# Reordering the first four attention steps of a fused dilated attention and gated unit kernel

## The chip, the cores and the metric

The kernel runs on one core of one Trainium2 chip. The metric is the device time of one execution in microseconds (us); of several runs of one kernel the median is given.

## The reference

The inputs q, k and v have 8 batches, 8 heads, 576 positions and 64 elements a head, in float32. Heads 0 to 3 attend to the last 32 positions; heads 4 to 7 attend to every fourth of the last 128. The heads' outputs are laid side by side and go through a gated unit with a causal convolution of 5 taps.

```python
scores = scale * q @ k^T                       # per batch and head, 576 x 576
mask_plain = (rel >= 0) & (rel < 32)           # heads 0-3
mask_dil = (rel >= 0) & (rel < 128) & (rel % 4 == 0)   # heads 4-7
attn = softmax(where(mask, scores, -1e9))
x = concat_heads(attn @ v)                     # 8 x 576 x 512
gate = sigmoid(causal_depthwise_conv(x, conv_w))       # 5 taps, per channel
out = (gate * (x @ w_val)) @ w_out             # 8 x 576 x 512
```

## The kernel before, in words

The work is cut into 32 steps, i = 0 to 31. A step is a pair of heads of one batch; four steps make a batch, and its channels 128c to 128c+127 (c = i % 4) are the pair's output. Two pairs form a group g: even groups hold heads 0 to 3 (plain), odd groups heads 4 to 7 (dilated). pair_info gives batch, c, kind, group and the place a of the pair in its group. The order of instructions on every engine is the order in which the program issues them; no scheduler changes it, and the queues are first in, first out.

Loads go through SP's queue in the order of issue (load_main for the first 512 positions of k or q, load_rest for the other 64, load_v for v). Groups 0 and 1 are loaded ahead of the loop, half of group 0's q by ACT's queue; groups 2 and 3 by pairs in steps 0 to 3, group 4 in step 3, and each later group two or so steps apart, three groups ahead. The pool of k_nat, q_nat and qk_rest has four buffers of each name. conv_w (conv_nat, 10 KB) is loaded by GpSimd's queue, as are w_val (step 1) and w_out (step 3), which are cast on the way.

Plain k and q are first cast to bf16 and reordered (cast, L171): group 0's first pair by VectorE (k) and ScalarE (q), its second pair by ScalarE inside step 0, and later groups by GpSimd, where these casts stand in one queue with the casts of v for dilated steps (prep_v, L183: vA and vB). In particular the casts of group 4's k are issued in step 4 and prep_v(6) in step 5.

trans_main (L321) transposes k or q of one or both pairs of a group on TensorE into a PSUM bank of the pool ps_one (four banks), and ScalarE copies the result out (for q of group 0: VectorE). trans_rest (L362) does so for the last 64 positions, with VectorE's copies. next_pair(i) (L579) does both for the pair of step i+1. From step 7 on, the transposes are made a whole group ahead.

A step runs scores (L390: for each half hf 6 matmuls into ps_sc, of which there are two, then an exp on ScalarE), apply_mask (L417: VectorE multiplies the exponentials by the mask), attn_v (L425: 6 matmuls of each half; both halves write into the ps_sc of half 1), and normalize (L446: reciprocal and product on VectorE). scores(i+1, 1) needs the ps_sc that normalize(i) reads. In the step after, after_x (L588) transposes the result (trans_x, VectorE copies it to xT) and appends two convolutions of the chunk to a list; pop_conv (L569) issues the first of that list when it is due. The convolution (L490) is a sum of matmuls with diagonal weights conv_diag[c], made by make_conv_diag(c) (L308) on VectorE from ident and conv_w_sb; setup_conv_w (L298) gets conv_w_sb by four small transposes on TensorE. run_val, val (L519) and out_tile (L535) are the products with w_val and w_out; they begin with steps 4 and 6. warm(n) (L573) issues n matmuls on constant data whose result is not used; they stand at the start and in steps 0 to 3.

make_mask_d builds the mask of dilated steps on GpSimd at the start, finish_mask_d ends it on VectorE in step 0. EARLY is 7, NCH is 4.

The softmax here doesn't subtract the row's maximum and nothing guards it: scores larger than these inputs give would overflow.

## Time and profile before

| what | value |
| --- | --- |
| median of 6 runs | 185.12 us (182.31 to 186.0) |
| the profiled execution | 182.72 us |
| its span in the profile | 181.0 us |
| PE (matmul) busy | 164.4 us, 91% |
| VectorE (DVE) busy | 119.0 us, 66% |
| ScalarE (ACT) busy | 120.4 us, 67% |
| GpSimd (POOL) busy | 42.0 us, 23% |
| moved by DMA | 42.28 MB, 234 GB/s over the span |
| start of scores(i, 0), i = 0 to 6 | 8.95, 13.34, 18.21, 22.98, 27.58, 32.32, 36.96 us |

All times in the profile are counted from the start of the span. PEld is TensorE's loading of weights. L508 is line 508 of the kernel. "SPq" and "ACTq" are the instructions with which SP and ACT issue DMAs; "out<-in" names the tile that is written and those that are read. A line of a timeline has start, duration, engine, line, operation, tiles, shape and count; the bracket at its end gives the idle time of the engine before it and what ended it. A slice is a fortieth of the span, here 4.525 us, and a digit the busy share in tenths.

### The profile page before, as it was taken

What the parts mean: (1) busy time and instruction counts of PE and PEld (TensorE: products, weight loads), DVE (VectorE), ACT (ScalarE), POOL (GpSimd) and SP (SyncE); (2) the same over time, 40 slices, a digit from 0 to 9 for tenths busy, and PEclk for the clock granted to TensorE, in tenths of its full rate; (3) what the DMA queues carried; (4) which work ended last, traced back from release to release, by engine and by line L of the source; (5) the groups of instructions that cost most, each with busy time, mean ns of one, the idle gap of its engine ahead of it and who ended that gap; (6) DMA issues with size and microseconds to landing.
All of it is one profiled execution on the core that took longest, in us unless ns stands there. A gap on an engine that the chain in (4) does not pass through costs nothing.

```text
span 181.0 us, 5175 instructions
## 1 busy us (share of the span) xinstructions
PE 164.4 (91%) x2029; PEld 119.7 (66%) x2057; DVE 119.0 (66%) x283; ACT 120.4 (67%) x217; POOL 42.0 (23%) x88
## 2 busy tenths in 40 slices
PE   5786777879999999999999999999999999999990
PEld 1445555657777777777777776777777777776650
DVE  3587466775677767577877776677877766774430
ACT  3266666658777777877877777777777778653341
POOL 6706420054054005300350054003600500000000
PEclk9999999999999999999999999999999999999999
DMA  5999999999999999999999999999997213112345
GB/s 151 259 277 307 217 251 302 304 268 283 329 268 229 295 327 267 211 314 325 279 246 286 332 277 216 319 316 287 217 296 258 71 58 116 62 58 63 116 126 163
DMA packets 62632, 42.28 MB, mean 234 GB/s; under 512 B 31371, under 2 KB 57995, under 8 KB 62608
## 3 DMA queue, kind: packets, MB, share of 16 engines
q1 hardware_dynamic: 60976, 40.57, 84.0%
q0 software_dynamic: 1088, 1.06, 3.6%
q8 instruction: 16, 0.26, 0.6%
q10 hardware_dynamic: 544, 0.33, 0.6%
q14 instruction: 8, 0.07, 0.1%
HBM read 33.56 MB, written 9.44 MB: 238 GB/s over the span
## 4 chain that ended last, share of the span: by engine, by line
PE 74%; SPq 11%; DMA 9%; issue 1%; POOL 1%; ACT 0%; DVE 0%; POOLq 0%; ACTq 0%
PE ps_bank L508 19%; PE ps_bank L538 17%; PE ps_bank L523 16%; SPq L115 7%; PE ps_bank L332 6%; PE ps_sc L441 6%; PE ps_sc L411 5%; DMA qk_rest<-in_k_dram 4%; DMA k_nat<-in_k_dram 3%; DMA q_nat<-in_q_dram 3%; PE ps_bank L469 2%; PE ps_bank L482 2%; SPq L148 1%; PE ps_bank L476 1%; PE ps_bank L367 1%
## 5 line engine op out<-in xcount | busy, mean ns | idle before, releaser
L508 PE MATMUL ps_bank<-xT,conv_diag 128*128 128x288 bf16 (+1 forms) x384 | 50.1, 266 | 2.0 <-DVE xT L484 2.0
L414 ACT ACTIVATE et<-ps_sc 128x576 bf16<-128x576 f32 x64 | 38.7, 648 | 6.7 <-PE ps_sc L411 4.2
L523 PE MATMUL ps_bank<-xT,w_val_b 128*128 128x288 bf16 x256 | 41.8, 286 | 0.4 <-DVE xT L484 0.4
L543 ACT ACTIVATE osb<-ps_bank 128x512 f32<-128x512 f32 x36 | 21.5, 597 | 25.1 <-PE ps_bank L538 21.8
L516 ACT ACTIVATE gate<-ps_bank 128x288 bf16<-128x288 f32 x64 | 26.7, 418 | 16.5 <-PE ps_bank L508 15.8
L508 PEld LDWEIGHTS <-conv_diag 128*128 128x128 bf16 x384 | 32.0, 97 | 8.4 <-issue 1.4
L529 DVE SCALAR_TENSOR_TENSOR y_all<-gate,ps_bank 128x288 bf16<-128x288 bf16 x64 | 28.9, 452 | 11.0 <-PE ps_bank L523 6.7
L538 PE MATMUL ps_bank<-w_out_b,y_all 128*128 128x512 bf16 x117 | 34.2, 379 | 1.4
L457 DVE TENSOR_TENSOR xn<-ps_sc,rec 96x768 bf16<-96x768 f32 (+1 forms) x32 | 30.6, 955 | 1.1
L523 PEld LDWEIGHTS <-w_val_b 128*128 128x128 bf16 x256 | 23.6, 98 | 10.1
L181 POOL CAST k_b<-k_nat 128x512 bf16<-128x512 f32 x14 | 8.9, 660 | 79.9 <-DMA k_nat<-in_k_dram 41.9
L441 PEld LDWEIGHTS <-et 128*128 128x128 bf16 x384 | 20.2, 98 | 5.2 <-DVE et L423 1.9
L452 DVE RECIPROCAL rec<-ps_sc 96x12 f32<-96x12 f32 (+1 forms) x32 | 7.4, 231 | 24.7 <-PE ps_sc L441 24.7
L484 DVE COPY xT<-ps_bank 128x576 bf16<-128x576 bf16 x32 | 14.6, 458 | 11.7 <-PE ps_bank L482 7.0
L538 PEld LDWEIGHTS <-y_all 128*128 128x128 bf16 x144 | 12.5, 97 | 10.9 <-DVE y_all L529 0.9
L423 DVE TENSOR_TENSOR et<-et,mask_p 128x576 bf16<-128x576 bf16 x32 | 15.9, 499 | 0.2 <-ACT et L414 0.2
L188 POOL CAST vA<-v_st 128x512 bf16<-128x512 f32 x16 | 10.9, 684 | 17.5 <-PE ps_sc L411 10.7
L423 DVE TENSOR_TENSOR et<-et,mask_d 128x576 bf16<-128x576 bf16 x32 | 15.0, 473 | 0.0
L441 PE MATMUL ps_sc<-vP,et 128*128 128x65 bf16 x192 | 11.4, 195 | 0.1
L347 ACT COPY kT<-ps_bank 128x1024 bf16<-128x1024 bf16 (+1 forms) x10 | 8.5, 848 | 4.2 <-PE ps_bank L332 4.2
L441 PE MATMUL ps_sc<-vA,et 128*128 128x65 bf16 x128 | 9.3, 194 | 0.4 <-POOL vA L188 0.4
L411 PE MATMUL ps_sc<-qT,kT 64*128 64x96 bf16 x192 | 7.5, 209 | 2.4 <-DVE qT L342 1.1
(82 smaller groups left out, 187.2 us busy)
## 6 DMA issues: line engine op xcount, KB each, us to landing
k_nat<-in_k_dram SPq DMA_DIRECT2D x12, 512.0 KB, 5.5
q_nat<-in_q_dram SPq DMA_DIRECT2D x12, 512.0 KB, 6.6
vP<-in_v_dram SPq DMA_DIRECT2D x6, 768.0 KB, 7.9
v_st<-in_v_dram SPq DMA_DIRECT2D x6, 512.0 KB, 6.5
k_nat<-in_k_dram SPq DMA_DIRECT2D x8, 256.0 KB, 5.0
out_dram<-osb SPq DMA_DIRECT2D x8, 256.0 KB, 5.3
q_nat<-in_q_dram SPq DMA_DIRECT2D x7, 256.0 KB, 5.2
out_dram<-osb SPq DMA_DIRECT2D x8, 224.0 KB, 3.6
```

What stands on the lines that cost most here:

```text
L411: nc.tensor.matmul(out=o, lhsT=lhsT, rhs=rhs, start=True, stop=True)
L414: nc.scalar.activation(out=e3, in_=ps[:, :, 0:HB], func=AF.Exp, scale=scale)
L423: nc.vector.tensor_tensor(out=e3, in0=e3, in1=m, op=ALU.mult)
L441: nc.tensor.matmul(out=ps[:, hf, x * AVS:x * AVS + D + 1], lhsT=et[:, hf, sl * HB + col:sl * HB + col + 128], rhs=rhs, start=True, stop=True)
L457: nc.vector.tensor_tensor(out=dst, in0=av[:, :, :, 0:D], in1=rec[0:R, :, :, None].to_broadcast([R, 2, 6, D]), op=ALU.mult)
L484: nc.vector.tensor_copy(xTs[b % NXT][:, c, :, 2:], pr)
L508: nc.tensor.matmul(out=ps[:, o * T:(o + n) * T], lhsT=conv_diag[:, c, K - 1 - m, :], rhs=xt[:, c, r:r + n, off:off + T], start=(idx == 0), ...
L516: nc.scalar.activation(out=gate, in_=ps[:, 0:HB], func=AF.Tanh, scale=0.5)
L523: nc.tensor.matmul(out=ps[:, 0:HB], lhsT=w_val_b[:, mc, c * 128:(c + 1) * 128], rhs=xt[:, mc, 2 * G:2 * G + 2, 2:], start=(mc == 0), stop= ...
L529: nc.vector.scalar_tensor_tensor(out=y_all[:, c, b * S + G * HB:b * S + (G + 1) * HB], in0=gates.pop((b, c, G)), scalar=1.0, in1=ps[:, 0:H ...
L538: nc.tensor.matmul(out=ps, lhsT=y_all[:, c, 128 * n:128 * n + 128], rhs=w_out_b[:, c, :], start=(c == 0), stop=(c == NCH - 1),)
L543: nc.scalar.mul(out=osb, in_=ps, mul=0.5)
```

## The change

conv_nat's load moves from GpSimd's queue to ACT's, behind the loads of q. At the start, all eight junk matmuls run together, then come the casts and transposes of the first pair, and only then setup_conv_w and the first diagonal set; the other three sets, which stood between the first transposes and in step 0, move to the ends of step 0 (set 1) and behind the second mask of steps 1 and 2 (sets 2 and 3). In steps 0 to 3 attn_v(i, 1) and normalize(i) follow attn_v(i, 0) at once. In steps 2 and 3 the transposes of the next pair stand before the first mask; in step 1 they stand behind normalize, and the second convolution of the step with them. One junk matmul of step 0 is gone. Steps 4 and later are as before.

```diff
-    nc.gpsimd.dma_start(out=conv_nat, in_=moe_conv_w)
     warm_in = consts.tile([1, 1], FP32, name="warm_in")
...
     load_v(0, 0, 2)
+    nc.scalar.dma_start(out=conv_nat, in_=moe_conv_w)
     nc.scalar.activation(out=warm_in, in_=warm_in, func=AF.Exp, scale=1.0)
...
-    warm(5)
+    warm(8)
+    cast(0, "k", 0, nc.vector)
+    cast(0, "q", 0, nc.scalar)
+    next_pair(-1)
     setup_conv_w()
     make_conv_diag(0)
-    warm(3)
-    cast(0, "k", 0, nc.vector)
-    cast(0, "q", 0, nc.scalar)
-    trans_main(0, "k", (0,))
-    make_conv_diag(1)
-    trans_main(0, "q", (0,))
-    trans_rest(0)
-    make_conv_diag(2)
     make_mask_d()
     make_perm()
     for i in range(NP):
...
             after_x(i - 1)
+        if 1 < i < NCH:
+            next_pair(i)
         if i >= EARLY and g + 1 < 2 * B:
             trans_main(g + 1, "k" if a == 0 else "q")
         apply_mask(i, 0)
...
         apply_mask(i, 1)
+        if 0 < i < 3:
+            make_conv_diag(i + 1)
         attn_v(i, 0)
-        if 0 < i < EARLY:
+        if i < NCH:
+            attn_v(i, 1)
+            normalize(i)
+        if i == 1 or NCH <= i < EARLY:
             next_pair(i)
         if i == EARLY - 1:
             trans_main(g + 1, "k")
         pop_conv(i + 0.5 if i >= NCH else i + 0.75)
-        if i == 0:
-            warm(1)
-        attn_v(i, 1)
-        normalize(i)
+        if i >= NCH:
+            attn_v(i, 1)
+            normalize(i)
         if i == 0:
             next_pair(0)
-            make_conv_diag(3)
+            make_conv_diag(1)
             finish_mask_d()
```

## The prediction

> **What bounds the kernel now.** I began with the page's busy shares and slices. PE is busy 164.4 of 181.0 us, but its first nine slices (40.7 us) stand at 5 to 8 tenths and all later ones near 9, while the DMA row stands at 9 from the second slice to the thirtieth. So there are two stretches, and the change lies in the first.

> ```profile
> PE   5786777879999999999999999999999999999990
> ...
> DMA  5999999999999999999999999999997213112345
> ```

> I then asked which of the two paths that run through the first 41 us, attention steps or loads, ends last. The chain of waits in order of time (start, us, what) answers it: to 38 us it holds issues and landings alone, then two casts of GpSimd, and only from 40.8 us on matmuls.

> ```profile
> 11.52 4.58 DMA q_nat<-in_q_dram
> 16.11 2.97 SPq L115
> ...
> 25.82 6.87 DMA qk_rest<-in_k_dram
> 32.78 5.12 DMA k_nat<-in_k_dram
> 38.05 1.17 POOL k_b L181 x2
> 39.22 0.68 POOL vA L188
> 39.95 0.63 POOL vB L191
> 40.84 0.89 PE ps_bank L332 x16
> 41.73 0.62 PE ps_bank L508 x6
> ```

> The timeline of PE shows the meeting point, in step i=6 (idle time before and its releaser in brackets):

> ```profile
> 38.83 0.78 PE L508 MATMUL ps_bank<-xT,conv_diag 128*128 128x288 bf16 x6
> 40.05 0.29 PE L441 MATMUL ps_sc<-vA,et 128*128 128x65 bf16 x4 [0.43 <-POOL vA L188]
> 40.62 0.22 PE L441 MATMUL ps_sc<-vB,et 128*128 128x65 bf16 x2 [0.28 <-POOL vB L191]
> 40.68 0.38 PE L332 MATMUL ps_bank<-ident,k_nat 128*128 128x128 bf16 x4
> ```

> attn_v(6, 0) waits 0.71 us for vA and vB. GpSimd makes them behind the two casts of group 4's k (issued at i=4, before prep_v(6) of i=5), and these wait for k's landing at 37.90. Nothing of compute holds that landing back. SP issues its loads in program order, each on the completion of the eighth before it (k_nat at 32.78 follows qk_rest's landing at 32.69), and the buffers of group 4 were free long before: group 0's last cast ended at 11.6. DMA moved 250 to 300 GB/s in each 5 us from 5 to 40. From 44 to 176 us PE is busy 130.45 of 132.00 us, so after this point time is PE's queue and cannot shrink by what stands before it.

> [...] vA's cast took 0.84 us and vB's 0.62 under the masks at 38.9 to 40.3, but 0.61 and 0.40 at 16.92 and 17.47. [...] Here the 128x512 junk matmuls start 0.43 us apart up to 10.4 us and 0.22 apart at 12.0.

> **Start-up.** Before, k_b's cast (6.91 on VectorE) stood behind conv_w_sb and the first diagonal set, which waited for PE, which waited for conv_nat and ident5. k landed at 4.27, so the cast sat ready for 2.6 us. Now eight junk matmuls run on, 1.56 + 8 x 0.427 = 5.0; k's cast ends at about 4.7; k's transposes start at 5.0 instead of 7.40; q_b is cast at 4.85 to 5.47, so q's end at about 6.1; qT's copy (0.42) ends at 6.6 instead of 8.89. The conv_w transposes now stand ahead of scores(0, 0). conv_nat leaves the ACT queue after the two q loads, at about 2.1 us; with 3.8 us to landing (its row) to 4.1 (the ACT row of qk_rest), it lands at 5.9 to 6.2, and four transposes of 0.56 us end by 6.8. scores(0) start at 6.8 instead of 8.95: 2.1 us earlier. The table load on ACT starts 0.5 to 0.7 us later, ends at 4.2, and is hidden by q's landing at 4.83. GpSimd's queue loses 0.66 us of issue; ident is needed at 5.0 and was ready at 2.6.

> **Diagonal sets.** Four stay four, about 0.82 us each. Sets 1 and 2 no longer stand ahead of qT's copy and the first masks. Set 1 takes set 3's place ahead of finish_mask_d (0.57 + 0.31 + 0.19). Sets 2 and 3 go behind the second mask of steps 1 and 2, while PE does 0.7 us of attn_v; about 0.3 us of each then delays normalize. That has no cover in its step, so I charge 0.6 us.

> **Steps 0 to 3.** In steps 1 to 3 attn_v(i, 1) stood behind two or three transposes groups (0.45 to 0.56 us) and a conv (0.62). With these moved, normalize follows attn_v(i, 0) by 0.2 us instead of 1.3: 1.1 us less on the loop scores, exp, mask, attn_v, normalize, trans_x, in each of three steps, less the 0.6. The transposes of steps 2 and 3 come before the mask, where PE waited for VectorE anyway (0.66 and 0.65 us idle at 20.4 and 25.2); their copies on ACT are before the gates, not after. One junk matmul (0.22 to 0.43) goes. I count 2.1 + 3 x 1.1 - 0.6 - about 1.2 for copies, casts and waits that then end last = 3.6 us: scores(4) at 24.0 instead of 27.58. From both sides: at least 2.1 (start-up alone), at most 5.4. No DMA of SP or weights moves in its queue; w_val_b, issued at 14.78 and 8.3 us on the way, is there at 23.1, and the first val comes at about 25.5.

> **Where the gain goes.** Step 4's transposes of q wait for the second q of group 2: landing 26.77, cast 0.62, so 27.45 instead of 30.70; 3.25 us are left. Step 5's trans_rest waits for group 3's q rest, which landed at 32.91 and was used at 35.44: 2.5 us are left. At step 6 the convs before attn_v end at 39.62 - 2.5 = 37.1, and vA isn't there. k lands at 37.90 as before; two casts end at 39.2, vA at 39.8, vB at 40.2. VectorE's masks are over by then, so the casts run their free 0.61 and 0.40: 0.4 us earlier than 40.58, and this is all that stays. The 0.71 us stall grows to about 2.8. Later loads keep their slack: group 5's k landed at 45.74, used at 49.48.

> Sum against the profiled execution: span 181.0 - 0.4 = 180.6, with its 1.7 us around it 182.3. The six runs' median, 185.12, is 2.4 us above that execution; the same subtraction gives **184.7 us**.

> **Rivals.**
> 1. *The floor is less firm than one profile shows.* The runs spread from 182.31 to 186.0. If the slower ones lose their 2.4 us in steps 0 to 5 [...], a lead of 2.5 us covers it, and the median becomes the floor's 182.3. If group 4 also lands earlier, up to the whole lead of 2.5 stays: 179.8 from the profiled run, 182.2 from the median. For: the stall before is only 0.71 us, so little more makes compute last. Against: in the profiled run, itself one of the fast ones, the chain to 38 us is DMA alone.
> 2. *PE's clock falls back in the stall (slower).* Place: before attn_v(6, 0). [...] 185.12 - 0.4 + 1.7 = 186.4. [...]
> 3. *conv_nat is late.* It now holds up PE's queue: scores(0) and everything behind them wait for the conv_w transposes. Each us after 6.2 moves the steps one for one; it reaches the end only when lead (2.5) and old stall (0.7) are used up, after about 9.5 us, and costs 2% from about 13. 186 to 189.
> 4. *The change does not do what it says:* the reordered steps gain nothing because ACT's copies (0.59 each) end last. Start-up's 2.1 us alone still beat the floor: 184.7 again. So the end cannot tell it; the steps' starts do.

> **How the numbers follow.** Floor with the median's spread (with rival 4): 0.60, 184.7, own range 184.0 to 185.6. Rival 1: 0.26, 182.2 to 182.3, of which half I let reach beyond 2%, as both parts may come together (179.8). Rival 2: 0.09. Rival 3: 0.05. About 2% is what a measurement of this kernel can tell from no change. Faster by over 2% (below 181.4): 0.13. Slower by over 2% (above 188.8): 0.05. Within: 0.82. The range of 8 in 10 takes the floor case, the larger part of rival 1 and most of rival 2: 181.3 to 186.6.

> **What would show it.** Right: scores(0) at 6.8, scores(4) near 24 (between 22 and 25.5), k of group 4 landing at 37.9 +- 0.5, an idle PE of 2 to 3.5 us before attn_v(6, 0) with GpSimd as releaser, and equal distances from there to the end. Wrong: a landing of group 4 that moved with compute; matmuls of the step after the stall at double length; scores(0) after 8; or an end more than 1 us earlier than the floor at step 6 allows.

## The result and the profile after

The changed kernel took 184.21 us in the median of 31 runs, the kernel before 183.73 us of 68, and the ratio is 1.0032 (95% interval 1.0012 to 1.0053): 0.3% slower, where 184.7 against 185.12, 0.2% faster, was forecast. Ratios here and below compare executions within 1.5% of the fastest of their kernel; the profiled one, 185.90 us, lies outside, so a second profile of the same kernel (after_again, 183.30 us, span 181.6) is read beside it.

The slices of the first profile (tenths of the span of 184.2 us; PEclk is the granted clock):

```profile
PE   6769876938999999999999999999999999999990
...
PEclk9999997996999999999999999999999999999998
DMA  4999998999999999989998999899999223112345
```

The first five slices of PE are together fuller than before, as the steps come earlier; then two are poor (6 at the seventh, 3 at the ninth), and PEclk, which was 9 throughout before, shows 7 at the seventh and 6 at the tenth. Loads still fill DMA to the same place.

The chain of waits of after_again (start, us, what), around the place where the chain of before turned from loads to matmuls:

```profile
31.47 5.97 DMA k_nat<-in_k_dram
37.59 1.17 POOL k_b L181 x2
38.76 0.42 POOL vA L188
39.26 0.41 POOL vB L191
39.72 0.22 PE ps_sc L441 x2
39.94 1.62 PE ps_bank L332 x16
41.56 1.20 PE ps_bank L508 x6
```

The order is that of before: landing of group 4's k, casts, attn_v(6, 0). What differs is at its end: the 16 transposes stand with 1.62 us where they had 0.89, and the six matmuls of the convolution with 1.20 where they had 0.62. PE's timeline of the same execution shows why:

```profile
34.90 0.78 PE L508 MATMUL ps_bank<-xT,conv_diag 128*128 128x288 bf16 x6
39.37 0.29 PE L441 MATMUL ps_sc<-vA,et 128*128 128x65 bf16 x4 [3.69 <-POOL vA L188]
39.72 0.22 PE L441 MATMUL ps_sc<-vB,et 128*128 128x65 bf16 x2
39.78 0.51 PE L332 MATMUL ps_bank<-ident,k_nat 128*128 128x128 bf16 x4
40.08 0.63 PE L332 MATMUL ps_bank<-ident,q_nat 128*128 128x128 bf16 x4
...
41.36 1.41 PE L508 MATMUL ps_bank<-xT,conv_diag 128*128 128x288 bf16 x6
```

PE had done the work ahead of attn_v(6, 0) 3.9 us earlier than before (the convolution ahead of the wait starts at 34.90 instead of 38.83), and waited 3.69 us instead of 0.71. Soon after, a group takes up to twice its time of before (the convolution behind the transposes 1.41 instead of 0.79). The windows of one us each show what PE was granted (columns: stretch, length, busy PE, PEld, DVE, ACT, POOL, PEclk, DMA share, GB/s):

```profile
39.00:40.00 1.00, 0.57 (x10) 0.47 (x10) 0.00 (x0) 0.00 (x0) 1.00 (x3) 0.95 1.41 227
40.00:41.00 1.00, 1.00 (x12) 1.00 (x11) 0.00 (x0) 0.68 (x2) 1.00 (x3) 0.50 1.07 183
...
42.00:43.00 1.00, 1.00 (x12) 0.74 (x10) 0.00 (x0) 1.00 (x2) 0.00 (x0) 0.50 0.36 62
43.00:44.00 1.00, 1.00 (x8) 0.55 (x6) 0.83 (x2) 0.30 (x1) 0.00 (x0) 0.84 0.51 155
```

The granted clock is 0.50 from 39.90 to 43.31 us, 3.41 us. In the first profile there are two such stretches, from 29.48 and from 43.13 us, 3.41 us each. The second follows the wait before attn_v(6, 0), the first a wait of 1.79 us in step 4, for group 2's q. The wait of step 4 and the fall behind it used up most of the lead: the wait before attn_v(6, 0) begins at 39.03 us there, before at 39.62.

### The profile page after: what moved, and what is told of

It is laid out like the page before. It is cut to its first block, busy times and chain, and to the rows that moved or that the text cites. A ratio compares the mean times of both kernels' runs of the same rounds, so it can differ in the third digit from the quotient of the medians.

```text
span 184.2 us, 5167 instructions
## 1 busy us (share of the span) xinstructions
PE 166.8 (91%) x2027; PEld 120.3 (65%) x2056; DVE 118.4 (64%) x283; ACT 120.3 (65%) x217; POOL 39.2 (21%) x87
## 4 chain that ended last, share of the span: by engine, by line
PE 75%; DMA 14%; SPq 3%; issue 2%; POOL 2%; ACT 1%; ACTq 0%; DVE 0%; POOLq 0%
PE ps_bank L508 19%; PE ps_bank L538 17%; PE ps_bank L523 16%; DMA k_nat<-in_k_dram 9%; PE ps_bank L332 6%; PE ps_sc L441 6%; PE ps_sc L411 5%; DMA q_nat<-in_q_dram 3%; DMA qk_rest<-in_q_dram 3%; PE ps_bank L469 2%; PE ps_bank L482 2%; SPq L115 2%; PE ps_bank L476 1%; POOL k_b L181 1%; PE ps_bank L367 1%
## 5 line engine op out<-in xcount | busy, mean ns | idle before, releaser
L508 PE MATMUL ps_bank<-xT,conv_diag 128*128 128x288 bf16 (+1 forms) x384 | 51.3, 270 | 1.0 <-DVE xT L484 0.8
L523 PE MATMUL ps_bank<-xT,w_val_b 128*128 128x288 bf16 x256 | 42.4, 289 | 0.4 <-DVE xT L484 0.4
L508 PEld LDWEIGHTS <-conv_diag 128*128 128x128 bf16 x384 | 32.6, 98 | 7.4 <-issue 1.4
L538 PE MATMUL ps_bank<-w_out_b,y_all 128*128 128x512 bf16 x117 | 35.2, 385 | 1.6 <-issue 0.2
L181 POOL CAST k_b<-k_nat 128x512 bf16<-128x512 f32 x14 | 8.8, 651 | 84.1 <-DMA k_nat<-in_k_dram 69.5
L441 PEld LDWEIGHTS <-et 128*128 128x128 bf16 x384 | 20.1, 99 | 8.4 <-issue 3.0
L188 POOL CAST vA<-v_st 128x512 bf16<-128x512 f32 x16 | 10.5, 659 | 17.7 <-DMA v_st<-in_v_dram 9.3
L441 PE MATMUL ps_sc<-vA,et 128*128 128x65 bf16 x128 | 9.3, 196 | 3.0 <-POOL vA L188 2.8
L441 PE MATMUL ps_sc<-vP,et 128*128 128x65 bf16 x192 | 11.3, 196 | 0.6 <-DVE et L423 0.4
L354 ACT COPY kA<-ps_bank 128x1024 bf16<-128x1024 bf16 (+1 forms) x10 | 8.5, 846 | 3.3 <-PE ps_bank L332 3.3
```

The source lines that it names most:

```text
L441: nc.tensor.matmul(out=ps[:, hf, x * AVS:x * AVS + D + 1], lhsT=et[:, hf, sl * HB + col:sl * HB + col + 128], rhs=rhs, start=True, stop=True)
L508: nc.tensor.matmul(out=ps[:, o * T:(o + n) * T], lhsT=conv_diag[:, c, K - 1 - m, :], rhs=xt[:, c, r:r + n, off:off + T], start=(idx == 0), ...
L523: nc.tensor.matmul(out=ps[:, 0:HB], lhsT=w_val_b[:, mc, c * 128:(c + 1) * 128], rhs=xt[:, mc, 2 * G:2 * G + 2, 2:], start=(mc == 0), stop= ...
L538: nc.tensor.matmul(out=ps, lhsT=y_all[:, c, 128 * n:128 * n + 128], rhs=w_out_b[:, c, :], start=(c == 0), stop=(c == NCH - 1),)
```

## The experiments

Theory 1: the lead in the steps ends at step 6, as the forecast had it, because group 4's k lands when it lands; but the wait that it turns into is long enough for PE's clock to fall to half, and that costs more than the change leaves. Theory 2, the rival of the first four runs: loads come later in the changed kernel, above all because conv_nat's load moved to another queue, and the clock is a by-product. Later runs name their own rival.

**Both kernels again.** No edit.

> The kernel before, unchanged, for a second profile of it. Theory 1 (PE's clock): no window of half clock between 5 and 175 us after the start-up, or one at most, PE idle before attn_v(6, 0) under 1.5 us. Theory 2 (loads): k of group 4 lands at 37.9 +- 0.4 us, as in the first profile. Ratio to the kernel before 1.000 +- 0.002.

> The changed kernel, unchanged, for a second profile of it beside the kernel before on one chip. Theory 1: PE idle 1.5 to 3 us before attn_v(6, 0), then a window of about 3.4 us at half clock, which costs about 1.7 us less what the shorter casts give (0.4); ratio 1.003 +- 0.002. Theory 2: group 4's k lands 1 us or more later than in the kernel before run beside it, and this alone makes the ratio.

before_again: 0.999 (0.9957 to 1.0023). after_again: 1.0042 (1.0015 to 1.007). Two profiles of each kernel and three of the experiments below, with times in us; the last column is what a landing costs until the next step starts, free of when the load came:

| profile | k of group 4 lands | PE idle before attn_v(6, 0) | clock halved behind it | scores(7) | landing to scores(7) |
| --- | --- | --- | --- | --- | --- |
| before | 37.90 | 0.71 | no | 43.95 | 6.05 |
| before_again | 39.53 | 1.64 | no | 45.36 | 5.83 |
| after | 39.87 | 2.77 | yes | 47.12 | 7.25 |
| after_again | 37.44 | 3.69 | yes | 44.66 | 7.22 |
| conv_nat_gpsimd | 37.14 | 2.79 | no | 42.74 | 5.60 |
| conv_nat_gpsimd_again | 39.48 | 1.78 | no | 45.31 | 5.83 |
| fill_stalls | 37.78 | filled | no | 43.39 | 5.61 |

The landing moves by about 2 us from one execution to the next in either kernel; my 37.9 +- 0.4 for before_again was too narrow, its wait of 1.64 us was longer than the 1.5 expected, and after_again's 3.69 longer than 3. Theory 2 does not explain after_again: its k landed earlier than both of before, and its step 7 starts 7.22 us later, not about 6. So few landings can't exclude that they come a little later on average. The granted clock per execution agrees with theory 1: in the set that after_again shares with before_again, 50 of 59 executions of the kernel before have a mean clock of 0.992 or more, and 1 of 22 of the changed one; of the 32 executions that the result lists, 2. This mean tells that the clock fell, not where: 3.41 us at half clock take about 0.009 from it wherever they lie.

**conv_nat's load back on GpSimd's queue.**

```diff
+    nc.gpsimd.dma_start(out=conv_nat, in_=moe_conv_w)
     warm_in = consts.tile([1, 1], FP32, name="warm_in")
...
-    nc.scalar.dma_start(out=conv_nat, in_=moe_conv_w)
```

> The changed kernel with the load of conv_nat put back on GpSimd's queue, at the front. Theory 1: this touches neither wait, so the ratio stays 1.003 +- 0.002 and the half-clock window behind step 6 stays. Theory 2 (on ACT's queue this load takes one of the completion slots that SP's issues wait for, so that all later loads come later): group 4's k lands as in the kernel before and the ratio is 0.997 to 1.000.

> conv_nat_gpsimd a second time, since six executions gave no interval. Theory 1: ratio to the kernel before 1.001 to 1.006, granted clock under 0.992 in most executions. Theory 2: 0.997 to 1.000, clock as in the kernel before.

What theory 2 rests on is in the traces: of SP's 165 DMAs in before none starts ahead of the landing of the eighth before it, and in after conv_nat's load, issued by ACT at 2.07 us, takes one of the eight semaphores that these use in turn.

The first run had six executions, too few for an interval: median 184.25 against 183.35, five of six below a clock of 0.992. The second: 1.0013 (0.9981 to 1.0045), 20 of 22 below it. The ratio alone doesn't tell the theories apart, its interval holds both; the clock does, it falls as in the changed kernel.

Theory 1's place was missed, though: neither profile of this kernel shows half clock behind step 6. In that of the second run it was halved from 27.85 to 34.67 us, behind a wait of step 4:

```profile
28.96 0.61 PE L332 MATMUL ps_bank<-ident,q_b 128*128 128x128 bf16 x4 [2.63 <-POOL q_b L181]
29.36 1.41 PE L508 MATMUL ps_bank<-xT,conv_diag 128*128 128x288 bf16 x6
...
41.64 0.29 PE L441 MATMUL ps_sc<-vA,et 128*128 128x65 bf16 x4 [1.78 <-POOL vA L188]
...
42.94 0.79 PE L508 MATMUL ps_bank<-xT,conv_diag 128*128 128x288 bf16 x6
```

This wait and fall used up the whole lead (scores(6) start at 37.20 us, before at 36.96). Behind step 6 the clock was full, and landing to scores(7) took 5.83 us, as in before_again. So not every execution with a low clock pays for it behind step 6.

The profiled execution of the first run is one in which the clock stayed full, and so it gives the price of a fall behind step 6. Its timeline of PE:

```profile
39.06 0.29 PE L441 MATMUL ps_sc<-vA,et 128*128 128x65 bf16 x4 [2.79 <-POOL vA L188]
39.41 0.22 PE L441 MATMUL ps_sc<-vB,et 128*128 128x65 bf16 x2
39.47 0.38 PE L332 MATMUL ps_bank<-ident,k_nat 128*128 128x128 bf16 x4
...
40.36 0.78 PE L508 MATMUL ps_bank<-xT,conv_diag 128*128 128x288 bf16 x6
```

A wait of 2.79 us, and yet the convolution takes 0.78: here the clock did not fall (1.00 granted from 36 to 48 us; the last section sets it beside after_again). From attn_v(6, 0) to scores(7) it needs 3.68 us (39.06 to 42.74), after_again 5.29 (39.37 to 44.66): one fall there costs 1.6 us. The times agree. Of the executions that such ratios compare, of the changed kernel and of this one together, 6 had a clock of 0.992 or more and a median of 182.06 us, 40 had 0.984 to 0.991 (about one stretch of 3.41 us) and 183.59, and 14 had 0.979 or less (about two) and 184.43. The six may in part be those whose loads came early.

**The waits filled.**

```diff
         trans_main(g, "k", (z,))
+        if i == NCH:
+            warm(7)
         trans_main(g, "q", (z,))
...
+        if i == EARLY - 1:
+            warm(12)
         attn_v(i, 0)
```

> The changed kernel with junk matmuls in the two places where PE waits for loads: 7 between the transposes of k and q in step 4 (about 1.5 us) and 12 ahead of attn_v(6, 0) (about 2.6 us). Theory 1 (the clock falls back in those waits): the granted clock stays full there, the steps behind step 6 take 4.7 us at once, and about 1.3 to 1.7 us come back: ratio to the kernel before 0.993 to 0.998. Theory 2 (the loads land later): PE waits for the loads as before, nothing comes back, ratio 1.002 to 1.005.

0.9986 (0.9957 to 1.0015), 21 of 22 executions at 0.992 or more. Against after_again's 1.0042 this is 0.56% back, some 1.0 us, less than the 1.3 to 1.7 us that theory 1 expected, and against the kernel before the point lies just above its range; it is clear of theory 2's. The two fillings were not run apart. Its timeline of PE:

```profile
36.81 2.75 PE L575 MATMUL ps_bank<-junk 128*128 128x512 bf16 x12
39.71 0.29 PE L441 MATMUL ps_sc<-vA,et 128*128 128x65 bf16 x4
...
41.01 0.79 PE L508 MATMUL ps_bank<-xT,conv_diag 128*128 128x288 bf16 x6
```

Junk work, whose result nothing uses, makes the kernel shorter here (0.9986 against 1.0042): with it PE's granted clock is 1.00 from 36 to 44 us, around the start of attn_v(6, 0).

**A longer wait without any lead.** The kernel before, with three copies on GpSimd into a tile that nothing reads:

```diff
+    scratch = consts.tile([128, 512], BF16, name="scratch")
...
             cast(g2, "k" if a == 0 else "q", 2, nc.gpsimd)
+            if i == NCH:
+                for _ in range(3):
+                    nc.gpsimd.tensor_copy(scratch, junk)
```

> The kernel before with three extra GpSimd copies of 128x512 (about 0.65 us each, 2.0 in all, into a tile that nothing reads) between the casts of group 4's k and that of v for step 6: PE's wait before attn_v(6, 0) becomes 2.7 to 3.6 us without any lead in the steps. Theory 1 (a wait of that length lets the clock fall back for 3.4 us, which costs 1.6 us): 2.0 + 1.6 us in most executions, ratio 1.016 to 1.021, granted clock 0.985 to 0.991. Theory 2 (the wait costs its length alone): 1.010 to 1.012, clock above 0.994.

1.0204 (1.0112 to 1.0295), from four executions, all below a clock of 0.986. The point is theory 1's, the lower end of the interval touches theory 2's. The profile (one line more stands above these functions, so L509 is the convolution) agrees with theory 1:

```profile
42.75 0.38 PE L442 MATMUL ps_sc<-vA,et 128*128 128x65 bf16 x4 [3.19 <-POOL vA L189]
...
44.86 1.40 PE L509 MATMUL ps_bank<-xT,conv_diag 128*128 128x288 bf16 x6
```

The clock was halved from 41.51 to 48.33 us, two stretches of 3.41 where theory 1 had one; the first began within the wait. Nothing else of the change is in this kernel, so in this execution a wait of 3.19 us was enough for the fall.

**The floor lifted.** In both kernels GpSimd casts v for steps 6 and 7 ahead of group 4's k, and TensorE makes all of group 4's transposes in step 7:

```diff
-        if i + 1 < NP:
+        if i == NCH:
+            prep_v(6)
+            prep_v(7)
+        elif i + 1 < NP and i not in (5, 6):
             prep_v(i + 1)
...
-        if i >= EARLY and g + 1 < 2 * B:
+        if i > EARLY and g + 1 < 2 * B:
             trans_main(g + 1, "k" if a == 0 else "q")
...
         attn_v(i, 0)
+        if i == EARLY:
+            trans_main(g + 1, "k")
+            trans_main(g + 1, "q")
+            trans_rest(g + 1)
...
-        if i == EARLY - 1:
-            trans_main(g + 1, "k")
...
-        elif i >= EARLY - 1 and a == 0 and g + 1 < 2 * B:
+        elif i >= EARLY and a == 0 and g + 1 < 2 * B:
```

> The kernel before with the meeting point at step 6 taken away: GpSimd casts v of steps 6 and 7 ahead of group 4's k, and TensorE makes group 4's transposes all in step 7 instead of steps 6 and 7. Theory 1 (the loads of group 4 are the floor, the steps are close behind it in this kernel): only the wait of 0.7 to 1.6 us goes, ratio 0.991 to 0.997. Theory 2 (step 6's wait costs nothing because PE's later queue absorbs it): ratio 1.000 +- 0.002.

> The changed kernel with the same two moves. Theory 1: its lead of 2 to 3 us now reaches the end, as far as later loads (group 5's k in step 8) allow; ratio to the kernel before 0.980 to 0.990, and lower than that of floor_lifted_before by 0.6 to 1.5%. The half-clock window behind step 6 goes, one may stay in step 4. Theory 2: no better than floor_lifted_before, 0.995 to 1.003.

> As floor_lifted_after, with 7 junk matmuls (about 1.5 us) between the transposes of k and q in step 4, where PE waits for GpSimd's cast of q. Theory 1: it takes away the half-clock window of step 4 in the executions that had one, and costs nothing where the wait is longer than 1.5 us; ratio equal to that of floor_lifted_after or up to 0.4% lower. Theory 2: junk matmuls are work like any other: 0.4 to 0.8% higher.

1.0004 (0.9963 to 1.0045) for the kernel before so lifted, 0.997 (0.9938 to 1.0001) for the changed one and 0.997 (0.9939 to 1.0002) for it with the seven junk matmuls: theory 1 missed on the first two, where the numbers are theory 2's. But the lead was there, and was given back later. The timelines of floor_lifted_after, first ScalarE, then PE:

```profile
71.79 0.96 ACT L516 ACTIVATE gate<-ps_bank 128x288 bf16<-128x288 f32 x2
78.23 0.60 ACT L543 ACTIVATE osb<-ps_bank 128x512 f32<-128x512 f32 x1 [5.49 <-DMA out_dram<-osb]
```

```profile
75.47 0.78 PE L508 MATMUL ps_bank<-xT,conv_diag 128*128 128x288 bf16 x6
80.06 0.38 PE L441 MATMUL ps_sc<-vA,et 128*128 128x65 bf16 x4 [3.81 <-ACT et L414]
```

Step 14 began at 73.89 us instead of 77.82, but ScalarE's copy of an output tile waited 5.49 us for one of the four buffers, whose output DMA stood behind loads in SP's queue (in before all 165 DMAs of this queue land in the order of issue); the exp of step 14 stood behind it, and PE waited 3.81 us. Its clock fell at 78.99 us, within this wait, and stayed halved for 6.83 us. The junk matmuls of step 4 changed nothing that can be measured, as theory 1 allowed. floor_lifted_before shows the same wait, 2.95 us before 81.62.

**The floor lifted, and eight buffers for output tiles.**

```diff
-    out_pool = ctx.enter_context(tc.tile_pool(name="osb", bufs=4))
+    out_pool = ctx.enter_context(tc.tile_pool(name="osb", bufs=8))
```

> floor_lifted_before with eight instead of four buffers of the output tile, so that ScalarE's copies of step 14 don't wait for output DMAs that stand behind loads. Theory 1 (its own steps bound it up to step 6, loads and outputs behind that): the wait of 2.9 us near 81 us goes; ratio to the kernel before 0.990 to 0.998. Theory 2 (the outputs' landing itself is the floor, not the number of buffers): ratio 0.999 to 1.003, with the wait moved.

> floor_lifted_after_fill4 (the changed kernel, lifted floor, 7 junk matmuls in step 4) with eight buffers of the output tile. Theory 1: the lead of 2 to 4 us reaches the end: ratio to the kernel before 0.978 to 0.988, below lifted_before_8osb by 0.8 to 1.5%; no wait of PE above 1 us between 40 and 175 us. Theory 2: the lead is lost to another wait on DMA, ratio 0.994 to 1.000.

> lifted_after_8osb without the 7 junk matmuls in step 4. Theory 1: where PE's wait for group 2's q in step 4 lets the clock fall back, 1.6 us are lost as far as later loads don't hide them; ratio 0.982 to 0.990, with more executions under a clock of 0.992 than with the junk matmuls. Theory 2: junk matmuls only cost; ratio 0.976 to 0.981.

0.9942 (0.9914 to 0.997) for the kernel before so lifted; 0.9825 (0.9775 to 0.9876) for the changed one with seven junk matmuls in step 4, and 0.9804 (0.9762 to 0.9846) without, both from six executions. Now theory 1's numbers hold, and the change is worth 1.2 to 1.4%, the difference of these ratios: 2.1 to 2.5 us of 183. The junk matmuls don't help here: without them the point is theory 2's and the clock of all six executions is full (0.994 to 1.0); the intervals overlap. One row of windows of the last kernel:

```profile
40.00:170.00 130.00, 129.57 (x1632) 95.68 (x1631) 91.08 (x207) 92.92 (x165) 25.62 (x46) 1.00 0.88 237
```

PE is busy 129.57 of 130.00 us at full clock: between 40 and 170 us hardly a wait is left in which the lead could go. This version beats both kernels: 179.47 us against 183.23 on its chip.

## Why the prediction was wrong

*Start-up: right.* scores(0) start at 7.14 and 6.58 us in the two profiles (forecast 6.8, before 8.95). conv_nat held nothing up: its transposes ran at 6.80 and 6.11. Rival 3 did not occur.

*Diagonal sets and steps 0 to 3: right in sum.* scores(4) start at 23.94 and 23.23 us; 24.0 was forecast. Rival 4 is out.

*Where the gain goes: right in its place.* The lead ends at attn_v(6, 0), with GpSimd as releaser. The landing of k was not the fixed 37.9 that I took it for; it spreads from 37.1 to 39.9 in these seven profiles. Nor was the lead that arrives there a fixed 2.5: it was 3.9 us in after_again, where step 4 had no wait for q, 0.6 in the first profile, where it had one of 1.79, and nothing in conv_nat_gpsimd_again. The shorter casts (vA 0.62 and vB 0.40 us in after_again) are seen where a lead arrives with a full clock: landing to scores(7) was 5.60 and 5.61 instead of 5.83 to 6.05, 0.2 to 0.4 us for the forecast 0.4.

*The step that failed* is the line "this is all that stays": it puts the fall of PE's clock at nothing, with rival 2 at 0.09. Rival 2 named the fall and its price: 1.7 us, measured 1.6. That price and the odds were assumed; no fall shows in the trace of before up to step 7, where the granted clock is 1.00. What was wrong was how likely the clock is to fall: I had given it one chance in ten. Of the stalls before attn_v(6, 0), those of 2.77 us (after), 3.69 (after_again) and 3.19 (delay_before) had a fall in them or up to 1.4 us behind them, one of 2.79 (conv_nat_gpsimd) had none. PE was not idle for all of the 3.41 us ahead of these falls: it was busy for 1.27, 0.47 and 1.45 us of them (last section). The stall of after_again was also longer than forecast, and step 4 has a second wait.

In 21 of 22 and 30 of 32 executions the clock fell somewhere. A rough sum takes 1.6 us in about 0.95 of the executions, less about 0.16 of the kernel before's (26 of 164 in all sets below 0.992), less 0.3 for the casts: 0.95 x 1.6 - 0.16 x 1.6 - 0.3 = 1.0 us slower. Measured were 0.3 to 0.4%, 0.6 to 0.8 us. The sum lets every fall cost its full price, and conv_nat_gpsimd_again shows one in step 4 that cost only lead; how many executions fell in which place stays open. So the sign turned on the chance of one term.

*Rival 1* named the spread of the runs, and put it in steps 0 to 5 of the kernel before. A lower clock goes with part of it: in the set of before_again, the kernel before's executions below 0.992 have a median of 185.77, those above of 183.03. The second part, that the change would cure it, was the reverse of what happened. What makes the rest of the spread, among executions at full clock (181.67 to 186.75), isn't settled; the landing's 2 us are in it.

*Range and median.* 184.21 lies in the range given, and near 184.7 by luck: the forecast's base, 185.12 from six runs, was 1.4 us high (68 runs have 183.73), and the change went the other way.

## What to carry to other kernels

A lead on a path that does not end last isn't free: it lengthens the wait at the meeting point, and in five profiles here TensorE's clock fell to half in or behind waits of 1.79 to 3.81 us. So price the wait that a gain turns into, and when it comes near 1.8 us, the shortest of these, fill it or move the meeting point. Lift one floor and look for the next at once; here a second one, output buffers behind loads, hid most of the gain until it went too.

## What the runs showed of the hardware

```profile
36.49:39.90 3.41, 0.47 (x9) 0.37 (x9) 0.00 (x0) 0.00 (x0) 2.31 (x5) 1.00 1.31 251
...
33.99:37.40 3.41, 1.77 (x22) 1.39 (x23) 2.37 (x6) 1.69 (x3) 0.12 (x1) 1.00 0.98 315
37.40:40.81 3.41, 1.69 (x27) 1.54 (x27) 0.00 (x0) 0.92 (x3) 3.40 (x7) 1.00 1.32 228
```

In after_again the wait lay mostly in one such stretch, PE was busy 0.47 us of it, and the clock fell at its end. In conv_nat_gpsimd the wait of 2.79 us is split at 37.40 us into 1.13 and 1.66, PE was busy 1.77 and 1.69 us, and the clock stayed full; that the split made the difference is my reading of this one execution. In the 3.41 us just ahead of seven falls PE was busy 0.47 us (after_again), 0.67 (floor_lifted_after), 1.06 (floor_lifted_after_fill4), 1.20 and 1.27 (after), 1.45 (delay_before) and 1.72 (lifted_after_8osb). No border between these and the 1.69 and 1.77 above is shown. First half-clock stretches of 3.41 us in which PE was busy 2.17 us (delay_before) and 2.34 (floor_lifted_after) were followed by a second one, those with 3.20 to 3.41 (after, after_again, floor_lifted_after_fill4, lifted_after_8osb) were not.
